# Memory attention plus SwiGLU on one core: the first step's tiles on other memory, a reciprocal kept in PSUM, a Silu call placed earlier, and a refitted order

## The chip, the cores and the metric

The kernel runs on one core of a Trainium2 chip. The time is device microseconds of one execution; the time before is the median of three runs. A profile of one execution gives the trace that is read here. The engines are named as the profile names them: PE (matmul), PEld (its weight loads), DVE (VectorE), ACT (ScalarE), POOL (GpSimd) and SP (SyncE, which issues the DMAs). Every engine executes its own queue in order.

## The reference

Sizes: 8 batches, 8 heads, 576 positions, head size 64, 32 memory slots; then 4608 tokens, model width 512, inner width 1536.

```python
a = phi - np.max(phi, axis=2, keepdims=True); a = np.exp(a)
a = a / (np.sum(a, axis=2, keepdims=True) + 1e-09)       # softmax over positions
k_m = np.einsum('bhsm,bhsd->bhmd', a, k)
v_m = np.einsum('bhsm,bhsd->bhmd', a, v)
scores = scale * np.matmul(q, k_m.transpose(0, 1, 3, 2))
attn = softmax over the 32 slots (with + 1e-09 on the sum)
x = np.matmul(attn, v_m)              # heads side by side: 4608 x 512
rms = np.sqrt(np.mean(x * x, axis=-1, keepdims=True) + 1e-06)
xn = x / rms * rms_g
out = (silu(xn @ w_gate) * (xn @ w_val)) @ w_out
```

The weights come as float64; the kernel turns them into float32 itself, and multiplies with each operand split into a high and a low float32r part.

## The kernel before, in words

The work has two parts, and the kernel never forms `x`: it multiplies the value memories with the weights first, and the attention weights with that product.

**Part 1** (the block under `with ExitStack() as c1`) does the attention. For each batch b: `prep` finds the maximum of phi and takes the exponentials into `e_bd`; `kv_steps` multiplies them with k and v into the PSUM tile `kvp` (L633), sums the exponentials by matmuls with `ones` into column 128 of the same tile (`sums`, L648), and then `post1` forms 1/sum in the small tile `si`, masks it with `hmask` into `im` and scales `kvp` by it (L656 to L665); `turn`, `post2`, `self_products` and `post3` transpose and give `km`, `vm` and the Gram matrix `gram`. For the pairs of batches 0 and 1, `q_steps` transposes q and `score_steps` makes the scores in the PSUM tiles `S` (two buffers of two banks each, last read by the subtraction in `top`, L786), their exponentials `ex` and the attention weights `a0` and `a1`. `x_steps` then transposes these (`tp`, PSUM tag "tr"), finds each row's mean square through the Gram matrix and scales the transposed weights by 1/rms into `ath` and `atl`; its scale `rp` is also a "tr" tile, read by L237. The scores of pairs 2 and 3 are made in part 2.

Beside it `convert` turns raw float64 weights into float32 (five DVE instructions, two or three on ACT, one or two on POOL) and splits them into `wh` and `wl`; chunk 0 of gate and value (`first_weights`) and chunk 1 (`second_weights`) are made in part 1. Chunk 1 lies on memory that the k, v and phi tiles leave.

**Part 2** is 48 steps. A step takes one pair of batches and one of the 12 chunks of 128 inner columns. `vw_steps` multiplies `vm` with the weights into `vp` (PSUM tag "vw", two banks, L974) and splits it to `xh` (ACT, L986) and `xl` (DVE, L987); `gv_steps` has 48 matmuls with `ath` and `atl` into `pg` and `pv` (L1010), Silu on ACT (L1018), the product `hf` on DVE (L1019) and its split `hh`, `hl`; every second step `out_steps` multiplies with the converted output weights into `po` (L1057), which is added to `acc` (L1065).

Memory: pools are laid out one after the other, tags in the order of their first request. When part 1's pools close, part 2's pools (`sb2`, `ps2`) take the same addresses. With `reuse_waits="tile"` a new tile waits only for the old tiles that it overlaps. In PSUM part 1's pool has the tags "tr" (2 banks), "kx" (2) and "S" (4), in this order; part 2's has "vw" (2), "g" (2), "v" (2) and "o" (2). So `vp` of step 0 lies on the two "tr" banks. In SBUF part 1's pool begins with `ones`, `hmask`, `a0` and `a1`, and part 2's begins with `xh` and `xl`.

Order: each step is a function with a place in a list (`ev`), and the list is sorted by numbers from the table `PRM`. What a function issues goes to a list scheduler with the place as its priority: in a timing model of its own, each engine takes the first instruction that is ready, so an instruction that is ready early can run far ahead of its place. The outcome is a fixed queue per engine. The loads of part 1 are chained (`load`) and keep their order on SP; weight conversions are kept behind the last urgent DVE instruction (`behind`). In `PRM`, `CE` says whether POOL or DVE makes `w` of the early weights, `SUM` who sums the score exponentials, `ESN` how many exponential tiles POOL adds ahead of the sums, `XE` who copies transposes; most of the rest are places in the order.

Of the kernel before, what the change touches and what calls it, by code (L numbers as in the profile page):

```python
# [19 lines left out]
WB = 4  # L20
PRM = dict(
    KB=4,
    QB=3,
    K_AT=[13.363, 15.05, 40.982, 65.819, 100.72, 121.436, 146.779, 167.28],
    KP=0.907,
    POST=[-0.317, -0.317, 4.032, 7.881, 15.383, 23.226],
    P1=4.2,
    PREP=[4.604, 5.96, 6.364, 6.4, 20.493],
    PD=[1.603, 10.918, 5.724, 18.42, 6.909, 0.895],
    EXP=[-1.616, 14.831, 1.92, 5.136, 15.121, 4.651],  # L30
    ES=1.147,
    PH=[9.097, 16.192, 41.396, 73.222, 103.794, 133.428],
    S_AT=[32.949, 48.182, 51.299, 66.888, 103.839, 110.401, 116.081, 122.952],
    KD=[-15.069, -115.131, -42.204, -7.345, -6.094, -15.243, -0.175, -2.835, -28.265, -16.354, -17.024,
        -8.311, -12.025, -12.235, -27.337, -21.619, -22.801, -22.01, -23.715, -24.999, -11.785, -13.845,
        -8.155, -10.419, -16.375, -22.685, -11.543, -19.501, -66.165, -9.755, -3.349, -20.028],
    QD=[6.956, 5.589, 2.612, 8.893, 23.53, 19.934, 25.06, 15.038],
    PD0=2.054,
    QL=3.761,
    OL=3.513,  # L40
    QO=[-1.164, 3.407, -1.815, -0.482, 0.012, 2.8],
    SO=[7.704, 15.319, 18.727, 24.931],
    X_AT=[100.47, 150.686],
    XP=1.802,
# [12 lines left out]
    RO=2.79,
    RS=5.688,
    RP=0.93,
    GV=[0.232, 0.271, 0.296, 0.752, 0.896, 1.089],  # L60
    VW=[-0.128, -0.088, 0.063],
    VW0=0.397,
    O=[0.116, 0.297, 0.448, 0.514, 0.879, 0.955, 1.365, 1.487, 1.518],
    PRE=[-0.634, 0.045, 0.27, 1.342, 2.044, 2.566],
    PRE0=[-0.813, 0.602, 1.228, 1.622, 2.25, 2.279],
    PI=0.128,
# [5 lines left out]
    XM=[22.486, 25.397],
    XN=[-0.337, -0.244, -0.081, 0.028, 0.132, 0.484, 0.518, 0.593, 0.593],
    LV=[20.239, 20.03, 20.406, 21.822],
    VD=[20.27, 15.694, 12.047, 24.508],
    U=[[-1.581, -1.57, -1.37, -1.197, -0.96, -0.96], [-1.522, -1.522, -1.12, -1.12, -1.036, -0.964], [-1.618,
        -1.5, -1.335, -1.085, -1.074, -0.071]],
# [23 lines left out]
def kernel(  # L101
# [376 lines left out]

    with ExitStack() as c1:
        sb = c1.enter_context(tc.tile_pool(name="sb1", bufs=2, reuse_waits="tile"))  # L480
        ps = c1.enter_context(tc.tile_pool(name="ps1", bufs=2, space=PSUM, reuse_waits="tile"))
        early_weights()
        c1k = ExitStack()
        sk = c1k.enter_context(tc.tile_pool(name="sbk", bufs=2, side="right", reuse_waits="tile"))

        ones = sb.tile([P, 1], F32, name="ones", bufs=1)
        nc.vector.memset(ones, 1.0)
        hmask = sb.tile([P, 2], F32, name="hmask", bufs=1)
        for g in range(4):
# [132 lines left out]
        def kv_steps(b):  # L622
# [112 lines left out]
        def q_steps(pr, s):  # L735
            def order():
                qt = st.pop(("q", pr, s))
                qr = sb.tile([P, NT, 2, 64], F32, tag="qr", name=f"qr{pr}_{s}")
                src, dst = qt.rearrange("p h (c d) -> p h c d", c=NT), qr.rearrange("p c h d -> p h c d")
                nc.scalar.copy(dst, src)  # L740
                st["qr", pr, s] = qr

            def turn(t0):
                n = min(4, NT - t0)

                def f():
                    if t0 == 0:
                        st["qT", pr, s] = sb.tile([P, NT, P], F32, tag="qT", name=f"qT{pr}_{s}")
# [16 lines left out]
        def score_steps(pr, s):  # L765
            R = 2 * NT

            def mm():
                qT = st.pop(("qT", pr, s))
                sp = ps.tile([P, 1024], F32, tag="S", name=f"S{pr}_{s}", bufs=PRM["B"][2])  # L770
                for t in range(NT):
# [9 lines left out]
            def top():  # L781
                spv = st.pop(("sp", pr, s))[:, :NT * 64].rearrange("p (r m) -> p r m", m=M)
                mxs = sb.tile([P, R, 1], F32, tag="mxs", name=f"mxs{pr}_{s}")
                nc.vector.tensor_reduce(out=mxs, in_=spv, axis=AX.X, op=ALU.max)
                ex = sb.tile([P, R, M], F32, tag="ex", name=f"ex{pr}_{s}", bufs=2)
                nc.vector.tensor_tensor(  # L786
# [8 lines left out]
            def norm():  # L795
# [5 lines left out]
                else:  # L801
# [462 lines left out]
```

## Time and profile before

| | |
|---|---|
| median of 3 runs | 883.67 us (882.39 to 885.04) |
| the profiled execution | 882.99 us; span of its instructions 881.2 us |
| mean granted TensorE clock | 0.978 |
| busy: PE, PEld, DVE, ACT, POOL | 835.1, 743.3, 547.5, 398.0, 309.7 us |
| DMA | 131.64 MB, mean 149 GB/s |

Part 1 fills about the first 140 us of the span; the first `vp` of part 2 starts at 139.88 us. Times inside the trace are counted from the span's start. "Idle before" in brackets is how long the engine stood still ahead of an instruction, and what released it. The granted clock is given as a share of full speed.

### The profile page before, as it was taken

The numbers are of one execution on the slowest core, as the hardware profiler recorded it, in microseconds if no ns is written. First come the engines' busy times: TensorE is split into PE (matmuls) and PEld (weight loads), VectorE is DVE, ScalarE is ACT, GpSimd is POOL, SyncE is SP. The second block draws the span as 40 slices with busy tenths as digits, with TensorE's granted clock in tenths as the row PEclk, the third lists the DMA queues.
The fourth block names the chain that finished last, engine by engine and source line by source line (L and its number), as shares of the span: only waits on it lengthen the run. The fifth ranks groups of instructions, "written<-read, shape, count | busy, mean of one in ns | idle before, by whom it ended". The sixth has DMA issues, their size and how long they took to land.

```text
span 881.2 us, 16498 instructions
## 1 busy us (share of the span) xinstructions
PE 835.1 (95%) x6207; PEld 743.3 (84%) x6207; DVE 547.5 (62%) x988; ACT 398.0 (45%) x709; POOL 309.7 (35%) x261
## 2 busy tenths in 40 slices
PE   5899898989999999999999999999999999999997
PEld 4787787979998978978889987979988898899896
DVE  5679684888578888897898636502443444444434
ACT  2656445767755555556545421435322323232220
POOL 2453525554534543533543621511221212122120
PEclk9989797999999999999999999999999999999999
DMA  9992934545435355344353464765645546453437
GB/s 322 326 386 72 299 110 102 154 139 147 122 78 136 119 135 149 111 122 134 115 149 102 141 155 113 192 167 133 176 103 148 133 119 173 105 148 82 90 100 169
DMA packets 110246, 131.64 MB, mean 149 GB/s; under 512 B 45140, under 2 KB 74840, under 8 KB 110168
## 3 DMA queue, kind: packets, MB, share of 16 engines
q1 hardware_dynamic: 110168, 130.60, 52.2%
q8 instruction: 49, 0.80, 0.4%
q14 instruction: 29, 0.24, 0.1%
HBM read 73.93 MB, written 31.46 MB: 120 GB/s over the span
## 4 chain that ended last, share of the span: by engine, by line
PE 65%; DVE 10%; DMA 8%; issue 6%; ACT 5%; POOL 4%; SPq 2%; ACTq 0%; POOLq 0%; DVEq 0%
PE po L1057 26%; PE pg L1010 12%; PE pv L1010 12%; PE kvp L633 3%; PE vp L974 3%; PE vq L924 2%; SPq L955 2%; POOL hl L1038 1%; DMA q<-in_q_dram 1%; PE kvp L648 1%; DMA xh<-sh 1%; ACT xh L986 1%; DVE ex L388 1%; DVE mi L418 1%; POOL w L434 1%
## 5 line engine op out<-in xcount | busy, mean ns | idle before, releaser
L1038 POOL TENSOR_TENSOR hl<-hf,hh 128x512 fp32r<-128x512 f32 (+1 forms) x86 | 125.7, 1464 | 284.6 <-ACT hh L1037 273.6
L1065 DVE TENSOR_TENSOR acc<-po,acc 128x512 f32<-128x512 f32 x180 | 123.3, 687 | 125.1 <-PE po L1057 124.0
L1057 PE MATMUL po<-oh,hh 128*128 128x512 f32 x387 | 155.7, 404 | 7.9 <-DVE acc L1065 3.0
L1057 PE MATMUL po<-ol,hh 128*128 128x512 f32 x387 | 153.0, 395 | 0.4 <-DMA xh<-sh 0.4
L1057 PE MATMUL po<-oh,hl 128*128 128x512 f32 x387 | 152.9, 395 | 0.0
L1019 DVE TENSOR_TENSOR hf<-pv,sg 128x256 f32<-128x256 f32 x192 | 84.4, 452 | 92.4 <-PE pv L1010 44.6
L1018 ACT ACTIVATE sg<-pg 128x256 f32<-128x256 f32 x192 | 77.0, 410 | 131.6 <-PE pg L1010 124.7
L1010 PE MATMUL pg<-ath,xh 128*128 128x320 f32 (+1 forms) x384 | 88.0, 302 | 6.8 <-ACT xh L986 4.4
L1057 PEld LDWEIGHTS po<-oh,hh 128*128 128x128 f32 x387 | 72.5, 188 | 23.3 <-DVE acc L1065 5.6
L1010 PE MATMUL pv<-ath,xh 128*128 128x320 f32 (+1 forms) x384 | 86.0, 300 | 1.3 <-DVE hf L1019 1.3
L1057 PEld LDWEIGHTS po<-oh,hl 128*128 128x128 f32 x387 | 72.8, 188 | 16.9
L1010 PE MATMUL pg<-ath,xl 128*128 128x320 f32 (+1 forms) x384 | 86.1, 297 | 1.0 <-DMA xl<-sl 0.9
L1010 PE MATMUL pv<-ath,xl 128*128 128x320 f32 (+1 forms) x384 | 86.5, 297 | 0.0
L1010 PE MATMUL pg<-atl,xh 128*128 128x320 f32 (+1 forms) x384 | 84.5, 296 | 0.0
L1010 PE MATMUL pv<-atl,xh 128*128 128x320 f32 (+1 forms) x384 | 84.4, 297 | 0.0
L1057 PEld LDWEIGHTS po<-ol,hh 128*128 128x128 f32 x387 | 72.9, 188 | 10.8 <-DMA ol<-od 1.6
L1037 ACT CAST hh<-hf 128x512 fp32r<-128x512 f32 (+1 forms) x86 | 57.6, 675 | 51.8 <-DVE hf L1019 38.1
L434 POOL TENSOR_TENSOR w<-mi,ex 128x512 f32<-128x512 f32 x34 | 43.9, 1291 | 91.1 <-ACT mi L425 56.7
L1010 PEld LDWEIGHTS pg<-ath,xh 128*128 128x128 f32 x384 | 64.5, 189 | 13.1 <-ACT xh L986 5.2
L987 DVE TENSOR_TENSOR xl<-vp,xh 64x1024 fp32r<-64x1024 f32 x48 | 58.5, 1219 | 18.5 <-ACT xh L986 17.8
L1010 PEld LDWEIGHTS pg<-ath,xl 128*128 128x128 f32 x384 | 64.4, 190 | 4.0 <-DMA xl<-sl 1.1
L1010 PEld LDWEIGHTS pv<-ath,xh 128*128 128x128 f32 x384 | 63.2, 190 | 4.8 <-DVE hf L1019 1.8
(148 smaller groups left out, 1540.3 us busy)
## 6 DMA issues: line engine op xcount, KB each, us to landing
xh<-sh SPq DMA_DIRECT2D x192, 64.0 KB, 2.1
xl<-sl SPq DMA_DIRECT2D x192, 64.0 KB, 2.0
out_dram<-acc SPq DMA_DIRECT2D x72, 128.0 KB, 2.4
raw<-in_moe_w_gate_dram SPq DMA_DIRECT2D x12, 512.0 KB, 4.0
raw<-in_moe_w_val_dram SPq DMA_DIRECT2D x12, 512.0 KB, 3.6
wd<-wh SPq DMA_DIRECT2D x24, 256.0 KB, 3.5
wd<-wl SPq DMA_DIRECT2D x24, 256.0 KB, 3.6
raw<-in_moe_w_out_dram SPq DMA_DIRECT2D x12, 512.0 KB, 3.6
```

What stands on the lines that cost most here:

```text
L434: (nc.gpsimd if on_pool else V).tensor_tensor(out=d["w"], in0=m, in1=ex, op=ALU.mult)
L633: nc.tensor.matmul(kvp[64 * par:64 * par + 64, cc, 0:128], e_bd[j][:, hp, c, :], st["kv", b, hp][:, :, 64 * c:64 * c + 64], start=(c == 0) ...
L924: nc.tensor.matmul(vp[:, h, e, :], vall[a][:, cc, k:k + 4, :].rearrange("p q m -> p (q m)"), w, start=(a == 0), stop=(a == 1),)
L974: nc.tensor.matmul(vp[:, cc, e, :], lhs(l), r[:, 2 * cc + e, :], start=(n == 0), stop=(n == 2),)
L987: urgent.append(nc.vector.tensor_tensor(out=xl[rows], in0=src, in1=xh[rows].bitcast(F32), op=ALU.subtract).ins)
L1010: nc.tensor.matmul(pt[:, :N], l[cc][:, b, half * P:half * P + P], r[:, cc, b, t0:t0 + n, :].rearrange("p t x -> p (t x)"), start=(m == 0), ...
L1018: nc.scalar.activation(sg[:, :N], pg[:, :N], AF.Silu)
L1019: urgent.append(nc.vector.tensor_tensor(out=hf[:, :, b, :], in0=pv[:, :N].rearrange("p (t x) -> p t x", x=64), in1=sg[:, :N].rearrange("p ...
L1037: nc.scalar.copy(hh, hv)
L1038: nc.gpsimd.tensor_tensor(out=hl, in0=hv, in1=hh.bitcast(F32), op=ALU.subtract)
L1057: nc.tensor.matmul(po, l[:, tt, :], r, start=(m == 0), stop=(m == 5))
L1065: nc.vector.tensor_tensor(out=accs[key], in0=po, in1=accs[key], op=ALU.add).ins
```

## The change

- **Pools.** A new SBUF pool `sb1a` lies ahead of `sb1` and holds `a0`, q, `qr`, `qT` and `ex`. A new PSUM pool `ps1s` with the "S" tiles lies ahead of `ps1`. `ones`, `hmask` and `rg` move to the persistent pool; `a1` is allocated when it is first written.
- **PSUM tags of part 2.** `pg` and `pv` get the tags "g0", "g1", "v0", "v1" with one buffer each, so that the banks in order are vw (2), g0, v0, g1, v1, o (2).
- **1/sum.** `si` is no tile of its own any more but column 129 of `kvp`.
- **Silu.** One activation with Silu on `ones` is placed at 150 in the order.
- **Order.** New numbers in `PRM`. The ones that change who does what: `CE[0]` 2 to 3 (POOL instead of DVE makes `w` of gate chunk 0), `SUM[1]` 0 to 2 (POOL instead of DVE sums one of eight score tiles), `ESN[6]` 0 to 1 (POOL adds two tiles ahead of batch 6's sums, 8 matmuls fewer), `XE[3]` 17 to 21 (one copy of pair 3 from DVE to ACT).

```diff
 PRM = dict(
+    DS=150,
...
-    K_AT=[13.363, 15.05, 40.982, 65.819, 100.72, 121.436, 146.779, 167.28],
-    KP=0.907,
-    POST=[-0.317, -0.317, 4.032, 7.881, 15.383, 23.226],
-    P1=4.2,
-    PREP=[4.604, 5.96, 6.364, 6.4, 20.493],
+    K_AT=[13.363, 15.05, 40.982, 64.708, 100.72, 121.436, 147.13, 167.28],
+    KP=0.88,
+    POST=[-0.317, -0.206, 4.032, 7.881, 15.383, 23.226],
+    P1=4.084,
+    PREP=[4.511, 5.867, 6.271, 6.307, 20.4],
...
-    EXP=[-1.616, 14.831, 1.92, 5.136, 15.121, 4.651],
+    EXP=[-9.517, 14.262, 1.741, 4.567, 14.552, 4.082],
...
-    CE=[2, 2],
-    XE=[12, 11, 29, 17],
-    ESN=[2, 3, 2, 0, 3, 1, 0, 1],
-    SUM=[2, 0, 1, 0, 0, 1, 2, 1],
+    CE=[3, 2],
+    XE=[12, 11, 29, 21],
+    ESN=[2, 3, 2, 0, 3, 1, 1, 1],
+    SUM=[2, 2, 1, 0, 0, 1, 2, 1],
...
     with ExitStack() as c1:
+        sa = c1.enter_context(tc.tile_pool(name="sb1a", bufs=2, reuse_waits="tile"))
         sb = c1.enter_context(tc.tile_pool(name="sb1", bufs=2, reuse_waits="tile"))
+        ps_s = c1.enter_context(tc.tile_pool(name="ps1s", bufs=2, space=PSUM, reuse_waits="tile"))
         ps = c1.enter_context(tc.tile_pool(name="ps1", bufs=2, space=PSUM, reuse_waits="tile"))
...
-        ones = sb.tile([P, 1], F32, name="ones", bufs=1)
+        ones = persist.tile([P, 1], F32, name="ones")
-        hmask = sb.tile([P, 2], F32, name="hmask", bufs=1)
+        hmask = persist.tile([P, 2], F32, name="hmask")
-        a_tiles = [sb.tile([P, NT, 256], F32, name=f"a{i}", bufs=1) for i in range(G)]
+        a_tiles = {0: sa.tile([P, NT, 256], F32, name="a0", bufs=1)}
-        rg = [sb.tile([P, HP], F32, name=f"rg{i}", bufs=1) for i in range(2)]
+        rg = [persist.tile([P, HP], F32, name=f"rg{i}") for i in range(2)]
...
-            t = sb.tile([P, 2, S], F32, tag="q", name=f"q{pr}_{s}", bufs=PRM["QB"])
+            t = sa.tile([P, 2, S], F32, tag="q", name=f"q{pr}_{s}", bufs=PRM["QB"])
...
-                si = sb.tile([P, 2, 1], F32, tag="si", name=f"si{b}")
+                si = kvp[:, :, 129:130]
...
-                sp = ps.tile([P, 1024], F32, tag="S", name=f"S{pr}_{s}", bufs=PRM["B"][2])
+                sp = ps_s.tile([P, 1024], F32, tag="S", name=f"S{pr}_{s}", bufs=PRM["B"][2])
...
+                if pr not in a_tiles:
+                    a_tiles[pr] = sb.tile([P, NT, 256], F32, name=f"a{pr}", bufs=1)
...
         ev += place(PRM["CV"], [PRM["CP"] * i for i in range(len(w))], w)
+        ev.append((PRM["DS"], lambda: nc.scalar.activation(
+            sb.tile([P, 1], F32, name="warm", bufs=1), ones, AF.Silu)))
...
-                    pg = ps.tile([P, 512], F32, tag="g", name=f"pg{i}_{gi}{b}")
-                    pv = ps.tile([P, 512], F32, tag="v", name=f"pv{i}_{gi}{b}")
+                    pg = ps.tile([P, 512], F32, tag=f"g{b}", name=f"pg{i}_{gi}{b}", bufs=1)
+                    pv = ps.tile([P, 512], F32, tag=f"v{b}", name=f"pv{i}_{gi}{b}", bufs=1)
```

The tiles `qr`, `qT` and `ex` of part 1 move to `sa` in the same way as q. The other changed numbers of `PRM` are places in the order, most of them by less than one unit.

More of the change, by code (lines that the diff above doesn't have):

```diff
@@ L21 @@
 PRM = dict(
+    DS=150,
     KB=4,
     QB=3,
-    K_AT=[13.363, 15.05, 40.982, 65.819, 100.72, 121.436, 146.779, 167.28],
-    KP=0.907,
-    POST=[-0.317, -0.317, 4.032, 7.881, 15.383, 23.226],
-    P1=4.2,
-    PREP=[4.604, 5.96, 6.364, 6.4, 20.493],
+    K_AT=[13.363, 15.05, 40.982, 64.708, 100.72, 121.436, 147.13, 167.28],
[3 more added lines that the diff above has]
+    PREP=[4.511, 5.867, 6.271, 6.307, 20.4],
     PD=[1.603, 10.918, 5.724, 18.42, 6.909, 0.895],
-    EXP=[-1.616, 14.831, 1.92, 5.136, 15.121, 4.651],
-    ES=1.147,
+    EXP=[-9.517, 14.262, 1.741, 4.567, 14.552, 4.082],
+    ES=1.541,
     PH=[9.097, 16.192, 41.396, 73.222, 103.794, 133.428],
-    S_AT=[32.949, 48.182, 51.299, 66.888, 103.839, 110.401, 116.081, 122.952],
+    S_AT=[32.949, 48.182, 51.299, 66.888, 103.621, 110.401, 116.081, 122.952],
     KD=[-15.069, -115.131, -42.204, -7.345, -6.094, -15.243, -0.175, -2.835, -28.265, -16.354, -17.024,
@@ L36 @@
         -8.155, -10.419, -16.375, -22.685, -11.543, -19.501, -66.165, -9.755, -3.349, -20.028],
-    QD=[6.956, 5.589, 2.612, 8.893, 23.53, 19.934, 25.06, 15.038],
-    PD0=2.054,
+    QD=[7.122, 5.589, 2.612, 8.893, 23.53, 19.934, 25.06, 15.038],
+    PD0=1.045,
     QL=3.761,
     OL=3.513,
[L41 to L44, printed above, removed]
+    QO=[-1.164, 3.407, -1.815, -0.482, 0.012, 2.591],
+    SO=[7.743, 14.98, 18.206, 24.112],
+    X_AT=[100.536, 150.686],
+    XP=1.796,
     LAG=0.891,
-    CV=112.01,
+    CV=111.332,
     CP=3.361,
     CV2=160.133,
-    CP2=1.082,
+    CP2=1.09,
     QE=[4, 0],
-    CE=[2, 2],
-    XE=[12, 11, 29, 17],
-    ESN=[2, 3, 2, 0, 3, 1, 0, 1],
-    SUM=[2, 0, 1, 0, 0, 1, 2, 1],
+    CE=[3, 2],
+    XE=[12, 11, 29, 21],
+    ESN=[2, 3, 2, 0, 3, 1, 1, 1],
+    SUM=[2, 2, 1, 0, 0, 1, 2, 1],
     CA=1,
@@ L57 @@
     RO=2.79,
[L58 to L66, printed above, removed]
+    RS=6.461,
+    RP=0.555,
+    GV=[0.232, 0.246, 0.274, 0.752, 0.884, 1.089],
+    VW=[-0.104, -0.023, 0.07],
+    VW0=0.373,
+    O=[0.116, 0.297, 0.452, 0.514, 0.874, 0.991, 1.365, 1.487, 1.518],
+    PRE=[-0.635, 0.045, 0.27, 1.342, 2.044, 2.566],
+    PRE0=[-0.813, 0.784, 1.109, 1.622, 2.25, 2.293],
+    PI=0.13,
     PSW=[1.981, 2.035, 1.951, 2.415, 3.159, 3.803],
-    SU=[1.874, 3.101, 5.773, 6.557, 9.723, 12.208, 13.41, 15.533],
-    AO=[0.214, 0.237, 0.237, 0.276, 0.394, 0.423, 0.543, 0.581, 0.621, 0.621, 0.621, 0.819, 1.065, 1.397],
+    SU=[1.877, 3.104, 5.776, 6.56, 9.726, 12.211, 13.413, 15.536],
+    AO=[0.214, 0.237, 0.237, 0.276, 0.397, 0.423, 0.543, 0.581, 0.621, 0.621, 0.621, 0.819, 1.065, 1.397],
     XB=[17.199, 22.761],
     XS=[0.1086, 0.0359],
[L72 to L77, printed above, removed]
+    XM=[22.138, 25.161],
+    XN=[-0.302, -0.244, -0.092, 0.028, 0.161, 0.484, 0.518, 0.593, 0.603],
+    LV=[20.282, 20.03, 20.406, 21.652],
+    VD=[29.86, 23.48, 21.637, 34.098],
+    U=[[-1.581, -1.578, -1.37, -1.197, -0.96, -0.96], [-1.522, -1.522, -1.12, -1.12, -1.036, -0.964], [-1.618,
+        -1.5, -1.335, -1.003, -1.003, -0.071]],
     RL=[-1.906, -3.752, -5.714],
-    RW=[1.932, 0.852],
+    RW=[1.932, 0.552],
     CB=1,
@@ L737, in order @@
                 qt = st.pop(("q", pr, s))
-                qr = sb.tile([P, NT, 2, 64], F32, tag="qr", name=f"qr{pr}_{s}")
+                qr = sa.tile([P, NT, 2, 64], F32, tag="qr", name=f"qr{pr}_{s}")
                 src, dst = qt.rearrange("p h (c d) -> p h c d", c=NT), qr.rearrange("p c h d -> p h c d")
@@ L747, in f @@
                     if t0 == 0:
-                        st["qT", pr, s] = sb.tile([P, NT, P], F32, tag="qT", name=f"qT{pr}_{s}")
+                        st["qT", pr, s] = sa.tile([P, NT, P], F32, tag="qT", name=f"qT{pr}_{s}")
                     qr = st["qr", pr, s]
@@ L784, in top @@
                 nc.vector.tensor_reduce(out=mxs, in_=spv, axis=AX.X, op=ALU.max)
-                ex = sb.tile([P, R, M], F32, tag="ex", name=f"ex{pr}_{s}", bufs=2)
+                ex = sa.tile([P, R, M], F32, tag="ex", name=f"ex{pr}_{s}", bufs=2)
                 nc.vector.tensor_tensor(
```

## Prediction

> **What bounds the kernel now.** I read the page first, then busy time by stretches of 4 us, then the stretch around the change from part 1 to part 2 engine by engine. The page:
>
> ```profile
> span 881.2 us, 16498 instructions
> PE 835.1 (95%) x6207; PEld 743.3 (84%) x6207; DVE 547.5 (62%) x988; ACT 398.0 (45%) x709; POOL 309.7 (35%) x261
> PEclk9989797999999999999999999999999999999999
> ```
>
> PE is busy 95% of the span, so 881.2 - 835.1 = 46.1 us is all that PE waits. The clock row, where a digit is a fortieth (22 us), shows less than full clock only in the first seven fortieths: what waiting and half clock cost early is found in part 1 and its end. The profiled execution took 882.99 us, 1.79 us more than its span; the median 883.67 lies 0.68 above that.
>
> Busy time by stretches (start:end, length, busy us and count of PE, PEld, DVE, ACT, POOL, then granted clock):
>
> ```profile
> 84.00:88.00 4.00, 2.35 (x39) 1.67 (x35) 4.00 (x11) 1.56 (x4) 2.01 (x3) 1.00 0.01 2
> 92.00:96.00 4.00, 2.15 (x16) 1.32 (x12) 3.74 (x15) 2.10 (x3) 1.81 (x5) 0.98 0.92 216
> 96.00:100.00 4.00, 1.68 (x22) 1.68 (x24) 0.00 (x0) 1.56 (x3) 1.16 (x1) 0.87 0.98 365
> 136.00:140.00 4.00, 3.41 (x22) 2.22 (x20) 3.73 (x8) 1.82 (x5) 1.12 (x3) 0.56 0.00 0
> 140.00:144.00 4.00, 2.81 (x12) 2.51 (x12) 0.12 (x1) 2.99 (x7) 4.00 (x4) 0.58 0.71 180
> 144.00:148.00 4.00, 1.80 (x10) 1.80 (x11) 2.89 (x4) 1.01 (x1) 2.49 (x4) 0.84 0.80 216
> 148.00:152.00 4.00, 4.00 (x28) 4.00 (x26) 2.25 (x5) 3.40 (x6) 1.29 (x1) 0.73 0.67 116
> 180.00:200.00 20.00, 16.30 (x97) 13.82 (x98) 16.47 (x23) 14.35 (x24) 10.68 (x8) 1.00 0.49 142
> ```
>
> From 136 to 152 us PE is busy for 12.0 of 16 us at 0.56 to 0.84 of its clock; from 92 to 100 for 3.8 of 8. Later idle stretches are single ones (3.70 us in 180 to 200). PE's own order shows what it waits for (the bracket is the idle time ahead of a row, and its releaser):
>
> ```profile
> 98.32 3.32 PE L633 MATMUL kvp<-kv,e_bd 128*64 128x128 f32 x33 [3.50 <-DMA kv<-in_v_dram]
> ...
> 138.42 0.47 PE L229 MATMUL rp<-ident,rinv 128*128 128x128 f32 x1 [0.28 <-DVE at L237]
> 139.88 0.58 PE L974 MATMUL vp<-wh,vm 128*128 128x256 f32 x1 [0.31 <-DVE at L237]
> ...
> 146.20 0.51 PE L1010 MATMUL pg<-ath,xh 128*128 128x256 f32 x2 [3.39 <-ACT xh L986]
> ...
> 149.79 0.57 PE L1010 MATMUL pv<-ath,xl 128*128 128x256 f32 x2
> ...
> 157.21 0.40 PE L1010 MATMUL pg<-ath,xh 128*128 128x256 f32 x2
> ```
>
> The first `vp` of part 2 waits for the DVE's L237 and then runs at half clock, PE stands still for 3.39 us until `xh` is there, and `pg` and `pv` of step 0 run at half clock until about 150.1 (4 us from 146.20). Step 1's `pg` begins at 157.21; I use that row as the mark by which the two kernels are compared. The hole ahead of 98.32 is another matter: a v tile of batch 5 that could not be loaded earlier; the change leaves the load's place (`KD`) as it is.
>
> **What the first step waits for, and what is left of it.** The DVE and POOL rows that decide:
>
> ```profile
> 89.58 0.75 DVE L786 TENSOR_TENSOR ex<-S,mxs 128x576 f32<-128x576 f32 x1
> ...
> 110.97 0.76 DVE L786 TENSOR_TENSOR ex<-S,mxs 128x576 f32<-128x576 f32 x1
> ...
> 137.16 2.67 DVE L237 TENSOR_TENSOR at<-at,rp 128x1024 f32<-128x1024 f32 x3
> ```
>
> ```profile
> 89.33 1.27 POOL L452 TENSOR_TENSOR wl<-w,wh 128x512 fp32r<-128x512 f32 x1 [0.73 <-ACT wh L451]
> ...
> 141.95 1.27 POOL L452 TENSOR_TENSOR wl<-w,wh 128x512 fp32r<-128x512 f32 x1
> ```
>
> Before, `vp` lies on the "tr" banks, whose last reader is the group of L237 that ends at 139.83. After, it lies on the first of the "S" buffers, whose last reader is the seventh score tile's L786 at 89.58 to 90.33; its weights' last piece `wl` is ready at 90.60. So `vp` of step 0 can start from about 91 us, and `xh`, `xl` on `a0` and q, dead by then, can follow at once (DVE is idle from 96 to 100). `pg` and `pv` of the first half lie on the other S buffer, free at 111.73, and those of the second half still on "tr". As the scheduler gives every engine whatever is ready, this work goes wherever PE has nothing else.
>
> That it runs instructions far ahead of their place is seen here: the copy of `gram` to `gb` for pair 0 has place 100.3 (`X_AT` less a tenth of `XP`), batch 1's `gram` has 43.7, and the copy ran 0.28 us behind it.
>
> ```profile
> 38.44 0.25 ACT L716 COPY gram<-kvt 128x128 f32<-128x128 f32 x1
> 38.72 0.82 ACT L198 COPY gb<-gram 64x256 f32<-64x256 f32 x2
> ```
>
> **The sum.** Term by term, against 882.99:
>
> The idle ahead of `pg` is removed: -3.39. The wait of `vp` for L237: -0.31; that of `rp` (0.28) stays, it lies on "tr" still. `vp` itself took 2.94 us there at half clock and 1.44 at full clock:
>
> ```profile
> 139.88 2.94 PE vp L974 x12
> 142.85 1.02 ACT xh L986
> 143.88 1.23 DVE xl L987
> ...
> 158.79 1.44 PE vp L974 x12
> ```
>
> In the hole of 3.50 us ahead of 98.32 it fits even at 2.94, and costs nothing: -2.94. The cover is the missing v tile; without the hole it costs 1.44 to 2.94 again, so this term lies between 0 and -2.94, and I take the end, since the hole's load keeps its order. Half clock from 146.20 to 150.1 costs half of 3.9 us, 1.95. It ends earlier if PE is kept busy from 137 on, but the sums before 136 and the rest of part 1 are still short matmuls: between 0 and -1.95, I take -1.0. Together -7.6.
>
> A second chain could hold the mark back: step 1's `vp` needs the `wl` that POOL ends at 143.22. Then 1.44 for `vp` and the 3.39 from `vp` to `pg`: 148.05, which is 9.2 us ahead of 157.21. That does not bind.
>
> [...]
>
> **What is handed back.** PE comes some 7 us early to the weight conversions. DVE is busy for 16.47 us of the 20 from 180 to 200, and PE waits 3.70 there. DVE has room ahead of that: 0.27 + 3.88 + 1.11 + 1.75 = 7.0 us idle in the four stretches from 136 to 152, and two `xl` (2.45) move out of them; the conversion of the first output weights, which is kept behind `xl`, can move up into that room. So most of the gain can hold. The ends are 0 and +3.7 (the wait of that later stretch once more); I take +1.0.
>
> **Moves that I cost at nothing.** 1/sum in PSUM: 3 DVE instructions for each of 8 batches now write or read PSUM. Nearest rows, PSUM to PSUM against PSUM to SBUF at 128x256:
>
> ```profile
> L284 DVE CUSTOM_DVE_ANT_0 xp<-xp,a 128x256 f32<-128x256 f32 x18 | 7.6, 429 | 1.7 <-PE xp L271 1.6
> ...
> L1148 DVE TENSOR_TENSOR ex<-S,mx 128x256 f32<-128x256 f32 x8 | 3.3, 416 | 0.1
> ```
>
> 13 ns more each, 0.3 us in all if every one were on the path; only batch 7's three are: 0.04. The other end, a cheaper write, is -0.3. The tags g0 to v1 keep the alternation of two buffers each; `ones`, `hmask`, `rg` change address only.
>
> Silu. The only table load ahead of Exp, the first Silu's load, and the last Exp of part 1:
>
> ```profile
> 3.88 1.28 ACT L602 ACT_TABLE_LOAD   x1 [3.88 <-DMA phi<-in_phi_dram]
> ...
> 117.11 2.34 ACT L602 ACTIVATE e_bd<-phi 64x1152 f32<-64x1152 f32 x2 [2.35 <-DVE phi L592]
> ...
> 149.82 1.28 ACT L1018 ACT_TABLE_LOAD   x1
> ```
>
> The new activation needs only `ones`, written in the first microsecond, so like the `gram` copy it will run at the front of ACT's queue; Exp is then loaded anyway at 3.88, in ACT's idle time, and the Silu load at 149.82 stays: 0. Ends: -1.28 if it came between the last Exp and the first Silu and the load was on the path; +2.56 if it ran just ahead of an Exp of batch 6 or 7 and both loads were on the path.
>
> POOL instead of DVE for `w` of gate chunk 0 takes one of these out of a stretch in which DVE is 4.00 of 4 busy and PE waits (84 to 88):
>
> ```profile
> 76.40 0.42 DVE L413 TENSOR_SCALAR mi<-raw 128x512 int32<-128x512 int32 x1
> ...
> 80.90 1.01 DVE L434 TENSOR_TENSOR w<-mi,ex 128x512 f32<-128x512 f32 x1
> ...
> 83.17 1.50 DVE L413 TENSOR_SCALAR mi<-raw 128x512 int32<-128x512 int32 x1
> ```
>
> ```profile
> 82.98 1.42 POOL L452 TENSOR_TENSOR wl<-w,wh 128x512 fp32r<-128x512 f32 x1 [0.39 <-ACT wh L451]
> ```
>
> -1.01 at most. But L413 took 0.42 at 76.40 and 1.50 at 83.17, beside a POOL instruction; a further POOL instruction of 1.3 us there can cost +1.08. I take 0 between these. [...] `SUM`, `ESN` and `XE` move work of the same size between engines that wait there; the other places shift what runs where by an amount that no row shows. I bound all that by the largest late idle stretch, won or lost once: 3.70 either way, and take 0.
>
> Sum: -7.6 + 1.0 = -6.6, so 876.4 for the profiled execution and 877.1 at the median. I predict 877.
>
> **The rivals.**
>
> *The gain is handed back at DVE.* PE is early, but `hf`, `xl` and the conversions from 150 to 200 are not. For it: 16.47 of 20 us. Against it: the idle DVE from 136 to 148. Price: +3.7 in place of +1.0, so 883.67 - 3.9 = 879.8; with a slightly worse order it falls into the middle band.
>
> *Slower: work of step 0 stands in PE's queue ahead of part 1's and waits.* The scheduler's model, not the chip, decides where `pg` of step 0 stands. If it stands among the batch 6 or pair 1 work from 108 to 129 and `xh`, `xl` are late on the chip, PE stops there as it did ahead of 146.20: 3.39, and then half clock for 3.9 us, 1.95: 5.3 us a time, on the chain that part 1 depends on. Once leaves -6.6 + 5.3 = -1.3; from the second time it is slower: 883.67 - 6.6 + 10.6 = 887.7. For it: PE's queue is in order, and a late load already holds it for 3.50 ahead of 98.32. Against it: after that hole `xl` has some 10 us to spare, until the second S buffer is free at 111.73.
>
> *The tiles do not come to lie so, or the model leaves the work where it was.* Then the handover stays, and only the refitted places act: 883.67 with 3.70 to either side.
>
> *The Silu stands late, ahead of the last Exp:* 877.1 + 2.6 = 879.7, still faster.
>
> **How the numbers follow.** The forecast, with the late Silu as a variant in it, has 0.66, and its own range is 871 to 881: with the clock at -1.95 and nothing handed back the sum gives 875.1, with a won stretch 871.4; with a lost one the forecast's 877.1 becomes 880.8. Handed back at DVE 0.15, slower by waiting 0.11, unchanged 0.08. A measurement can tell about 0.3% from no change here: faster is below 881.0, slower above 886.3. Of the rival at DVE I count half as faster, of the unchanged one a little on each side: faster 0.75, same 0.14, slower 0.11. The range for 8 in 10 goes from 870 to 885: it takes in the unchanged handover and the DVE rival, and leaves out the slower one and the far tail below.
>
> **What would show it.** In the changed kernel `vp` of step 0 stands before 100 us, or at least before the last sums; the idle of 3.39 ahead of the first `pg` is gone; the stretches from 136 to 152 show PE near 4 of 4 busy and full clock from about 142; step 1's `pg` begins near 150. The first Silu's table load is still there, beside a new one at the start. From 160 to 200 PE's idle grows by about 1 us, not 4. I am wrong if step 0's `vp` still follows L237, if PE shows a new wait for `xh` or `xl` inside part 1, or if the mark moves by 7 us and the end does not.

## The result and the profile after

The changed kernel takes 879.59 us (median of 16 runs, 875.54 to 882.89); the kernel before took 883.44 us beside it (16 runs, 879.5 to 889.34). The ratio is 0.9945 with an interval from 0.9923 to 0.9968: 4.9 us faster, by 2.8 to 6.8. (The means of the 16 runs give the same 0.9945; the medians differ by 3.9 us.) A ratio leaves out a run that lies over 1.5% above the fastest of its kernel, which happened once, in *numbers and 1/sum in PSUM* below (888.55 us). I had predicted 877.0, between 870 and 885, and faster. The sign and the range hold; the profiled execution even came out at the 876.4 us of my sum. It did so by another route than the sum's, and most of this section and the next is about that.

The page of the changed kernel:

```profile
span 874.6 us, 16472 instructions
PE 826.1 (94%) x6191; PEld 737.7 (84%) x6191; DVE 541.1 (62%) x985; ACT 398.4 (46%) x712; POOL 315.3 (36%) x268
PEclk9999797999999999999999999999999999999999
```

Span minus PE's busy time is 48.5 us, against 46.1 before. PE does not wait less. It is busy for 9.0 us less, with the same matmuls but for the 8 that `ESN[6]` saves (two records each: 6191 against 6207). Those are batch 6's sums, which take 2.90 us of PE in place of 3.85. What the page offers for part of the rest is the clock: the granted mean is 0.982 against 0.978.

PE's order at the two places that the prediction spoke of. Columns: start, length, then the instructions; in brackets the idle time ahead and what ended it:

```profile
92.74 2.61 PE L636 MATMUL kvp<-kv,e_bd 128*64 128x128 f32 x22 [2.90 <-DMA kv<-in_v_dram]
...
132.89 0.70 PE L710 MATMUL kvt<-vt 128*64 128x64 f32 x8
133.52 0.58 PE L981 MATMUL vp<-wh,vm 128*128 128x256 f32 x1
...
139.83 0.50 PE L1017 MATMUL pg<-ath,xh 128*128 128x256 f32 x2 [3.38 <-ACT xh L993]
...
150.38 0.40 PE L1017 MATMUL pg<-ath,xh 128*128 128x256 f32 x2
```

Here the forecast's mechanism falls. Step 0's `vp` has lost its wait, as the new tiles allow, but it did not move. It stands right behind part 1's last transposes (`kvt` from `vt`), and not in the hole ahead of 92.74. The idle time ahead of `pg` is 3.38 us, against 3.39 before. From `vp` to the first `pg` it is 6.31 us, against 6.32. Of the handover only the 0.31 us of `vp`'s wait is gone.

The mark, step 1's `pg`, is nevertheless at 150.38 in place of 157.21, 6.8 us earlier. But a second profile of the same changed kernel has it here:

```profile
104.86 0.48 PE L680 MATMUL kvt<-ident,kb 128*128 128x128 f32 x1
...
136.84 0.38 PE L981 MATMUL vp<-wh,vm 128*128 128x256 f32 x1
...
142.73 0.59 PE L1017 MATMUL pg<-ath,xh 128*128 128x256 f32 x2 [4.21 <-ACT xh L993]
...
153.27 0.40 PE L1017 MATMUL pg<-ath,xh 128*128 128x256 f32 x2
```

The mark moves by 2.9 us between two executions of one program, so one pair of profiles cannot say what an edit is worth here. The lead of 6.8 us has two parts, one that is the change and one that is chance. (0.4 us of it is order: four `qtp` records that stood ahead of the mark now stand behind it.) The stretches around 45 us show the part that is chance. Up to there PE's queue is the same in both kernels, and yet batch 2's transposes start at 48.37 us before, at 44.84 in the changed kernel's first profile, and at 47.45 in its second. Columns: start and end, length, busy time of PE, PEld, DVE, ACT and POOL, granted clock, DMA share and GB/s. The kernel before, the changed kernel, and its second profile:

```profile
40.92:44.34 3.42, 3.30 (x64) 3.08 (x59) 2.27 (x3) 3.37 (x5) 0.00 (x0) 1.00 1.05 391
44.34:47.75 3.41, 3.41 (x30) 2.63 (x32) 1.69 (x7) 2.53 (x4) 2.09 (x5) 0.50 1.06 383
47.75:51.16 3.41, 3.41 (x73) 2.88 (x71) 2.21 (x6) 1.67 (x6) 1.85 (x3) 1.00 1.07 384
```

```profile
44.97:48.38 3.41, 3.41 (x68) 2.95 (x69) 3.00 (x8) 1.82 (x6) 2.30 (x4) 1.00 1.05 379
```

```profile
44.01:47.42 3.41, 3.41 (x40) 2.88 (x40) 1.28 (x5) 2.12 (x3) 2.51 (x6) 0.50 1.04 380
```

In the kernel before, PE runs at exactly half clock from 44.34 to 47.75 and does 30 matmuls there, against 73 in the next 3.41 us. The changed kernel does not have this stretch in its first profile, and has it in its second. In the first 160 us the kernel before drew 37.5 us of half clock, the changed kernel 27.3 in one profile and 34.1 in the other. In the kernel before, step 0's `vp` took 2.94 us at half clock and step 1's 1.44 at full clock; from these I estimate that half clock costs half of its length where PE is busy throughout, and the first pair's difference of 10.2 us is worth up to 5.1 us. This is one reason why the first profile pair can show more (6.6 us) than the 16 runs each do (4.9).

Part 2 varies too. From the mark to the end of the span it is 723.99 us before, 724.22 and 720.63 in the two profiles of the changed kernel. PE's waits for the output weights account for 2.6 of the 3.6 us between the last two (tile and line, the releaser, then total, count and longest). First profile, from 150 us on:

```profile
PE po L1064 <- DMA oh<-od: 3.0, 3, 1.2
PE po L1064 <- DMA ol<-od: 2.1, 1, 2.1
```

Second profile:

```profile
PE po L1064 <- DMA oh<-od: 1.6, 2, 0.8
PE po L1064 <- DMA ol<-od: 0.9, 2, 0.5
```

The two rows hold 5.1 and 2.5 us.

### The profile page after: what moved, and what is told of

It reads as the page before. It is cut to its first block, busy times and chain, and to the rows that moved or that the text cites. A ratio compares the mean times of both kernels' runs of the same rounds, so it can differ in the third digit from the quotient of the medians.

```text
span 874.6 us, 16472 instructions
## 1 busy us (share of the span) xinstructions
PE 826.1 (94%) x6191; PEld 737.7 (84%) x6191; DVE 541.1 (62%) x985; ACT 398.4 (46%) x712; POOL 315.3 (36%) x268
## 4 chain that ended last, share of the span: by engine, by line
PE 71%; DVE 11%; DMA 5%; issue 4%; ACT 4%; POOL 3%; SPq 2%; POOLq 0%; ACTq 0%; DVEq 0%
PE po L1064 28%; PE pg L1017 14%; PE pv L1017 14%; PE vp L981 3%; PE vq L931 3%; PE kvp L636 2%; DMA q<-in_q_dram 1%; DVE ex L389 1%; POOL w L435 1%; PE kvp L651 1%; DVE mi L419 1%; DVE acc L1072 1%; POOL hl L1045 1%; DVE ex L392 1%; DVE xl L994 1%
## 5 line engine op out<-in xcount | busy, mean ns | idle before, releaser
L1064 PEld LDWEIGHTS po<-ol,hh 128*128 128x128 f32 x387 | 73.3, 189 | 11.9 <-DMA ol<-od 2.9
```

Of the source, the lines that this page charges most:

```text
L1064: nc.tensor.matmul(po, l[:, tt, :], r, start=(m == 0), stop=(m == 5))
```

## The experiments

Ratios are to the kernel before, run on the same chip beside each.

| kernel | ratio | interval | median us |
|---|---|---|---|
| changed kernel | 0.9945 | 0.9923 to 0.9968 | 879.59 |
| the same again | 0.9966 | 0.9939 to 0.9993 | 878.74 |
| numbers of `PRM` alone | 0.9980 | 0.9958 to 1.0003 | 881.25 |
| the same again | 0.9989 | 0.9968 to 1.0010 | 882.2 |
| all but the numbers | 0.9971 | 0.9944 to 0.9997 | 880.12 |
| the same again | 0.9967 | 0.9942 to 0.9992 | 880.28 |
| numbers and 1/sum in PSUM | 0.9919 | 0.9892 to 0.9946 | 878.55 |
| Silu call alone | 1.0012 | 0.9985 to 1.0039 | 882.72 |
| changed, without the Silu call | 0.9945 | 0.9912 to 0.9977 | 877.27 |
| changed, Silu call behind the last Exp | 0.9983 | 0.9961 to 1.0005 | 882.63 |
| changed, batch 5's last loads earlier | 1.0011 | 0.9985 to 1.0037 | 883.3 |
| changed, step 0's `vp` issued in part 1 | 0.9947 | 0.9922 to 0.9973 | 878.27 |
| the same, q loads ahead of others | 0.9944 | 0.9916 to 0.9973 | 876.46 |

### The change in two halves

My theory was the prediction's: the memory edits carry the gain. Its rival: the numbers carry it. *Numbers alone* is the kernel before with the changed table and no Silu call (two of the changed places):

```diff
-    K_AT=[13.363, 15.05, 40.982, 65.819, 100.72, 121.436, 146.779, 167.28],
+    K_AT=[13.363, 15.05, 40.982, 64.708, 100.72, 121.436, 147.13, 167.28],
...
-    CE=[2, 2],
+    CE=[3, 2],
```

> The kernel before with the whole table PRM of the changed kernel (without the place of the Silu call) and nothing else: pools, PSUM tags, 1/sum and Silu stay as before. Theory 'numbers' (the whole gain comes from the refitted places and assignments): the ratio of the changed kernel, 0.9945 (878.6 us against 883.44), within 0.001; in its trace step 1's first pg near 150.5 and the first vp near 133.5 with at most 0.3 us of wait for L237 ahead of it. Theory 'memory' (the gain comes from tiles on other addresses): 1.000, 883.4 us. Theory 'clock' (the two profiled runs differ mainly by how many half-clock stretches each happened to draw in part 1, 11 before and 8 after, and the order is worth little): between 0.995 and 1.000, and the trace again shows another set of half-clock stretches.

*All but the numbers* is the changed kernel with the table of before (pools, tags, 1/sum and the Silu call stay):

> The changed kernel with the table PRM of before (and the Silu call at 150): pools, PSUM tags, 1/sum in PSUM and the Silu call as changed, every engine's order as before except the Silu call at the front of ACT. Theory 'numbers': 0.9995 to 1.000 (at most 0.31 us for vp's wait for L237), about 883.2 us, and the idle of 3.4 us ahead of the first pg is still there. Theory 'memory': 0.9945, 878.6 us. My prediction's mechanism (vp floats into the hole near 98 us, 3.4 us of idle gone) would be 0.992 to 0.994 here; by the order of its queue vp stays behind the last kvt, so I do not expect it.

And the changed kernel once more beside them:

> The changed kernel unchanged, to set beside the other three on the same chip, and as a second trace of the same program. Theory 'numbers': 0.9945 again, and in the trace the same early lead as in the first (kvt of batch 1 at 27.6 against 29.6 before, kvt of batch 2 at 44.8 against 48.4), as it comes from the order. Theory 'clock': the order is the same in both kernels up to about 48 us, so the lead of 3.5 us at 44.8 is not the change's; this trace shows kvt of batch 2 anywhere between 44.8 and 48.4, and half-clock stretches at other times than the first trace.

The numbers alone give 0.9980, the rest 0.9971, the changed kernel 0.9966. The intervals overlap, so I ran both halves again:

> The kernel before with the changed kernel's numbers, a second time, to halve the interval (0.9958 to 1.0003 the first time). Theory 'numbers carry the gain': 0.996 or below. Theory 'a clean share of each': 0.998.

> The changed kernel with the numbers of before, a second time (0.9944 to 0.9997 the first time). By its queues only vp's wait for L237 (0.31 us) can go, so theory 'numbers': 0.9995 to 1.000. If it is 0.997 again, the memory edits do something that the order of the queues does not show.

They gave 0.9989 and 0.9967. The two means are 0.9985 and 0.9969, which are 1.3 and 2.7 us; multiplied they give 0.9954, between the two ratios of the changed kernel. So the halves add up within the uncertainty, and the memory half is the larger one by its means; each interval of its two runs excludes 1, and neither interval of the numbers does. This half has an instructive property: its queues hold the same instructions in the same order as those of the kernel before, but for the Silu call at ACT's front. Whatever it gains, it gains without an instruction having moved. Two things differ: the wait of `vp`, 0.31 us, and where the operands lie.

### What the memory half gains by

An instruction that I had passed over in the profile of before shows it. `im` is the mask times 1/sum, four elements wide. In DVE's order of the kernel before, four of its eight rows:

```profile
61.11 0.47 DVE L659 TENSOR_TENSOR im<-si,hmask 128x4 f32<-128x4 f32 x1
...
71.69 0.31 DVE L659 TENSOR_TENSOR im<-si,hmask 128x4 f32<-128x4 f32 x1
...
106.47 0.92 DVE L659 TENSOR_TENSOR im<-si,hmask 128x4 f32<-128x4 f32 x1
...
118.15 0.36 DVE L659 TENSOR_TENSOR im<-si,hmask 128x4 f32<-128x4 f32 x1
```

POOL's order of the same kernel:

```profile
70.72 1.27 POOL L614 TENSOR_TENSOR es<-e_bd 128x512 f32<-128x512 f32 x1 [3.21 <-ACT e_bd L602]
...
117.33 1.16 POOL L813 TENSOR_TENSOR a<-ex,sm 128x576 f32<-128x576 f32 x1 [3.85 <-DVE sm L812]
```

The second `im` ends at 72.00 and POOL's `es` at 71.99; the last `im` ends at 118.51 and POOL's `a` at 118.49. The other long ones end in the same way, 0.01 to 0.03 us behind a POOL instruction that was already running. The remaining four take 0.15 to 0.16 us. The sums of all eight, by groups of instructions on DVE (count, then total and mean ns of one, then idle time ahead): the kernel before, numbers alone, and the changed kernel:

```profile
L659 DVE TENSOR_TENSOR im<-si,hmask 128x4 f32<-128x4 f32 x8 | 2.7, 336 | 0.2
```

```profile
L660 DVE TENSOR_TENSOR im<-si,hmask 128x4 f32<-128x4 f32 x8 | 3.7, 468 | 0.2
```

```profile
L662 DVE TENSOR_TENSOR im<-kvp,hmask 128x4 f32<-128x4 f32 x8 | 1.3, 159 | 0.2
```

With 1/sum in SBUF both inputs of `im` lie there, and the group takes 2.7 to 3.7 us in four profiles. With 1/sum in PSUM it takes 1.3 us in all ten, and no single one takes more than 0.16. Every long `im` (0.31 to 1.18 us in place of 0.16) began behind the POOL instruction that it ends with, and none with one input in PSUM was held: at 57.30, 66.40, 101.45 and 111.78 in the changed kernel a POOL instruction ran beside `im`, which took 0.15 or 0.16 us. By what mechanism the long ones were held, no run shows.

The excess, 1.4 us before and 2.3 to 2.5 with the numbers alone, lies on a chain: sums, 1/sum, `im`, `kb` and `vb`, their transposes on PE. But in the profile of before PE waits for none of the eight `kb`, so the time may come back through what stands behind `im` in DVE's queue; by which wait it reaches the end no row shows. Two runs test whether it is this edit. First the Silu call alone, to take it out of the memory half; it is the kernel before with

```diff
+        ev.append((150, lambda: nc.scalar.activation(
+            sb.tile([P, 1], F32, name="warm", bufs=1), ones, AF.Silu)))
```

> The kernel before with one line more: the Silu call on ones, placed at 150, which runs at the front of ACT's queue (0.73 to 2.2 us) as in the changed kernel; every other engine's order is the same. So far the kernels with that call at the front were at 0.9945, 0.9966 (the changed kernel), 0.9971 and 0.9967 (memory edits with the old numbers), those without it at 0.998 and 0.9989 (numbers only) and 0.9983 (the call moved behind the last Exp). Theory 'the call at the front carries the gain of the memory edits': 0.997. Theory 'the tiles' addresses carry it' or 'chance': 1.000, since nothing in the trace waits for or gains by that call.

1.0012: the Silu call gives nothing. Then *numbers alone* with this one edit of memory, and neither pools nor tags:

```diff
-                si = sb.tile([P, 2, 1], F32, tag="si", name=f"si{b}")
+                si = kvp[:, :, 129:130]
```

> The kernel before with the changed kernel's numbers and 1/sum in column 129 of kvp; pools, PSUM tags and Silu stay as before. In every trace with 1/sum in SBUF so far (before, silu_only, numbers_only twice) three or four of the eight im instructions (im<-si,hmask) take 0.31 to 1.18 us in place of 0.16 and end 0.01 to 0.03 us behind a POOL instruction that runs beside them: 1.4 us too much in all with the old numbers, 2.3 to 2.5 with the new; with 1/sum in PSUM all eight take 0.15 or 0.16, in seven traces. Theory '1/sum in PSUM carries the gain of the memory edits': 0.9985 less about 0.0028, so 0.995 to 0.997, as the changed kernel; no im over 0.2 us. Theory 'pools and PSUM tags carry it': 0.998 to 0.999, though im is short.

0.9919, where the numbers alone had 0.9980 and 0.9989, with the same order on PE, DVE, POOL and SP; `im` takes 1.3 us again. The ratio stands on five runs; the median of all six (878.55 us, against 884.22 beside it) gives 0.9936. From 0.9985 it is 5.8 us to the first and 4.3 to the second, with an uncertainty of about 3 us from the intervals, and the memory half, which holds the same edit, gave 2.7. The trace's excess of 2.3 to 2.5 us sits at the low end of the first two and close to the last. That the edit shortens `im` is shown, by all ten profiles that have it; that it makes the kernel faster is what these runs say together; whether it is worth 2.5 or 5 us is not settled. For the new pools and PSUM tags no gain is left that these runs could tell: the kernel with them is at 0.9945, the one without at 0.9919. They were not run by themselves.

### The Silu call

The changed kernel runs it at the front, ahead of Exp's table. ACT's order there and at part 2's first Silu:

```profile
0.73 1.28 ACT L880 ACT_TABLE_LOAD   x1 [0.73 <-PEq L1255]
2.02 0.20 ACT L880 ACTIVATE warm<-ones 128x1 f32<-128x1 f32 x1
3.83 1.28 ACT L605 ACT_TABLE_LOAD   x1 [1.60 <-DMA phi<-in_phi_dram]
...
143.45 1.28 ACT L1025 ACT_TABLE_LOAD   x1
144.75 0.66 ACT L1025 ACTIVATE sg<-pg 128x256 f32<-128x256 f32 x2
```

So the load ahead of the first Silu, at 143.45, stays. One end of the prediction's range said that the call would be worth 1.28 us between the last Exp and the first Silu. I put the call behind part 1's last Exp:

```diff
+        def warm():
+            with tc.issue_after(exps[-1]):
+                nc.scalar.activation(sb.tile([P, 1], F32, name="warm", bufs=1), ones, AF.Silu)
+
+        ev.append((169.0, warm))
```

> The changed kernel with the Silu call pinned behind part 1's last Exp on ACT, where ACT has idle time, in place of the front of ACT's queue; every other engine's order is the same. The Silu table is then loaded near 114 us and the first sg of part 2 has no load ahead of it. Theory 'the load at 143.45 is covered, PE has other matmuls until 146': 0 us, ratio as the changed kernel's, 0.9945 to 0.997, and step 1's first pg still 10.5 us behind step 0's. Rival 'the load is on the path': -1.28 us, and that distance becomes 9.3.

0.9983: nothing gained, and by its mean slower than the changed kernel (the intervals overlap). Its ACT order, and the row of PE that follows from it:

```profile
115.26 2.34 ACT L605 ACTIVATE e_bd<-phi 64x1152 f32<-64x1152 f32 x2 [2.35 <-DVE phi L595]
117.61 1.28 ACT L882 ACT_TABLE_LOAD   x1
118.91 0.20 ACT L882 ACTIVATE warm<-ones 128x1 f32<-128x1 f32 x1
119.02 0.57 ACT L220 COPY at<-tp 128x512 f32<-128x512 f32 x1
```

```profile
119.64 1.98 PE L272 MATMUL xp<-gb,at 128*64 128x128 f32 x16 [0.98 <-ACT at L220]
```

The load now stands ahead of the copy of `at`, and PE waits 0.98 us for it. Just ahead of that it waits 0.81 us for POOL; the two waits together are 1.79 us, against 1.53 and 1.76 in the two profiles of the changed kernel, so these rows show next to no loss. Nothing comes back at the other end: step 1's `pg` starts 10.5 us behind step 0's with the load at 143.45 as without it, so PE's other matmuls cover that load. Without the call at all,

```diff
-        ev.append((PRM["DS"], lambda: nc.scalar.activation(
-            sb.tile([P, 1], F32, name="warm", bufs=1), ones, AF.Silu)))
```

> The changed kernel without the Silu call; all else is the same, the order of PE, DVE, POOL and SP too. Theory 'the call at the front carries the gain of the memory edits': 0.9985 as numbers only. Theory 'addresses': 0.9955 as the changed kernel (0.9945 and 0.9966). Theory 'the Silu call is worth nothing', my prediction's: the same.

the kernel has 0.9945, the changed kernel's own ratio. The call is worth nothing where it is.

### The forecast's mechanism, put there by hand

Is it true that an early `vp` removes the idle time ahead of `pg`? I issued step 0's `vp`, `xh` and `xl` in part 1's own list, on the S tile as the change has it, behind the sums of batch 6; `qr` and `qT` share a pool with part 2's `xl` and `xh`:

```diff
+        sx = ctx.enter_context(tc.tile_pool(name="sbx", bufs=2, reuse_waits="tile"))
...
+            vp0.append(ps_s.tile([P, 1024], F32, tag="S", name="vp0", bufs=PRM["B"][2]))
...
+                        with tc.issue_after(last["sum", 6]):
+                            nc.tensor.matmul(
...
+        ev += [(159.5, early_mm), (176.5, early_split)]
...
-    ev = place(-1.0, PRM["VW"], vw_steps(0))
```

> The changed kernel, with step 0's vp, xh and xl issued from part 1's own list: vp takes an S tile and stands on PE behind the sums of batch 6, just ahead of the first tp of pair 1, which waits 1.53 us for POOL there; the two xh stand on ACT behind the copy of batch 6's gram (5.18 us idle behind it), the two xl on DVE behind the last rinv (3.46 us idle behind it). qr and qT share the memory of xl and xh. This does what I predicted of the change: vp out of the handover and no idle ahead of the first pg. Theory 'the forecast's mechanism is worth what I reckoned, only the change did not bring it about': the idle of 3.4 to 4.2 us ahead of pg goes, vp's 1.5 to 2.9 us go into a hole, the first pg starts within 0.5 us of the last kvt; against the changed kernel -5 to -7 us, 872 to 874 us, ratio to the kernel before 0.989 to 0.991. Rival 'the gain is handed back': step 1's xh, xl or wl, or DVE at 150 to 200 us, holds PE instead; less than 2 us is left, 0.9945 to 0.997.

PE's order of this kernel:

```profile
115.77 0.39 PE L893 MATMUL vp<-wh,vm 128*128 128x256 f32 x1
...
139.22 0.69 PE L712 MATMUL kvt<-vt 128*64 128x64 f32 x8 [1.36 <-ACT vt L696]
139.84 0.58 PE L1048 MATMUL pg<-ath,xh 128*128 128x256 f32 x1
...
149.67 0.50 PE L1048 MATMUL pg<-ath,xh 128*128 128x256 f32 x2
...
154.72 0.52 PE L1157 MATMUL qtp<-ident,qr 128*128 128x128 f32 x3 [2.88 <-DMA qr<-in_q_dram]
```

`vp` is 23 us ahead of the handover, and the first `pg` follows the last `kvt` with no idle time. From batch 5's transposes of `kb` (107.08 here) to step 1's `pg` it is 42.6 us, against 47.5 and 48.4 in the two profiles of the changed kernel. Seven matmul records that stood ahead of the mark now stand behind it (four of `qtp`, three of `po`, about 1 us), so I count records as well: when PE has 1665 of them behind it, the same work in each kernel, it is 38.7 us from batch 5's `kb` against 42.8 and 43.8. So the mechanism is real, and worth 4 to 5 us there, part of it less half clock (7.9 us between `kb` and the mark, against 13.7 and 10.8). Note that `pg`, whose inputs were ready at 133.3, still stands behind part 1's last transposes: instructions issued in part 2 did not pass the end of part 1's list in any of these kernels.

Yet the time is 0.9947. The last row above holds the answer for this kernel: PE, early, finds q of pair 2 not there, waits 2.88 us, and then runs 3.4 us at half clock. Counted in matmul records, at 1800 of them, it stands 62.3 us behind batch 5's `kb`, against 61.5 and 62.5 in the changed kernel: the lead is gone. The q loads were issued at 149.48, behind others on SP. I kept those others back:

```diff
+                    with tc.issue_after(pins["q", G, 0]):
+                        nc.sync.dma_start(
```

> The kernel with step 0's vp in part 1 (early_vp), with one thing more: the loads of vgl (L1127) are kept behind the first loads of q for pair 2 on SP. In early_vp's trace PE stood 2.88 us at 154.72 for that q, issued at 149.48, which the earlier start of part 2 had uncovered, and ran 3.4 us at half clock behind it; all other engines' orders stay. Theory 'the rest of the forecast's gain was lost there': q is issued 1.3 us earlier or more, the wait falls to about 1.5 us, and the half-clock stretch may go: 0.3 to 3 us less than early_vp's 0.9947, 0.992 to 0.994. Rival 'it is lost elsewhere in part 2': 0.9947 again.

```profile
152.93 0.63 PE L1158 MATMUL qtp<-ident,qr 128*128 128x128 f32 x4 [0.65 <-DMA qr<-in_q_dram]
```

The wait falls to 0.65 us, the path from batch 5 stays short (43.1 us), and the ratio is 0.9944. On the same chip the changed kernel without its Silu call has 0.9945. So 2.2 of the 2.88 us of that one wait were recovered and do not show in the time. The count of records tells where they go: at 1800 this kernel is 2.2 to 3.1 us ahead of the two profiles of the changed kernel, at 4000 (496 us of its span) still 2.4 to 3.3, and at 4800 1.3 ahead of the one and 0.6 behind the other. Over those 800 records PE waits 5.1 us for DMAs of weights and of `xl` and draws one piece of half clock. The changed kernel waits 5.0 us for such DMAs there in one profile and 2.6 in the other, so whether the early `vp` brings these waits about is open. No version came out faster than the changed kernel beyond the uncertainty.

### The hole ahead of batch 5's tile

The prediction had put `vp` into the hole that a late v tile of batch 5 leaves. What if the tile is loaded earlier?

```diff
-        -8.155, -10.419, -16.375, -22.685, -11.543, -19.501, -66.165, -9.755, -3.349, -20.028],
+        -8.155, -10.419, -16.375, -22.685, -11.543, -19.501, -20.0, -9.755, -3.349, -20.028],
```

> The changed kernel with one number more changed: KD[28] from -66.165 to -20, so that the first k and v tile of batch 7 no longer takes one of the four kv buffers ahead of batch 5's last tile. In the queue of SP batch 5's last tile and batch 6's loads then stand ahead of the stores of wh and wl (L464), which wait for POOL. Theory 'the hole of 2.90 us ahead of kvp at 92.74 is set by that load, issued only at 86.14 behind those stores': the hole goes and PE, which is busy 0.47 of 4 us from 88 to 92 and 3.26 at half clock from 92 to 96, gains 3 to 6 us: 873 to 876 us, ratio 0.988 to 0.992. Rival 'DVE sets the end of that stretch' (4.00 busy of 4 from 76 to 84): the time comes back as waits for DVE or POOL, at most 1 us gained, 0.994.

1.0011, so nothing gained, and by its mean the changed kernel's gain is lost (the interval touches that of the changed kernel's second run). The trace is of the slowest of its 12 runs (890.01 us), so I read the order of the waits in it and not their sizes. The tile is issued at 63.40 in place of 86.14 and the wait for it is gone, but PE's order and the stretches of this kernel show another wait in its place:

```profile
89.12 0.79 PE L272 MATMUL xp<-gb,at 128*64 128x128 f32 x8 [2.89 <-DVE ssq L285]
```

```profile
84.00:88.00 4.00, 1.70 (x23) 1.03 (x18) 4.00 (x5) 1.41 (x3) 2.38 (x3) 1.00 0.09 33
88.00:92.00 4.00, 2.46 (x24) 2.09 (x26) 4.00 (x14) 1.67 (x4) 1.78 (x2) 0.69 0.01 2
92.00:96.00 4.00, 4.00 (x57) 3.66 (x55) 4.00 (x9) 1.60 (x3) 2.63 (x4) 0.88 0.79 210
```

DVE is busy for 12.0 of 12 us there, and in the changed kernel for 11.9 of the 12 from 76 to 88. That fits the rival, by which DVE sets the stretch with or without the tile; what else is lost here no run shows.

## Why the prediction was right, and where it was wrong

- **The step that failed:** "As the scheduler gives every engine whatever is ready, this work goes wherever PE has nothing else." The freed memory makes `vp` ready at about 86 us in the changed kernel (the seventh score tile is last read until 85.09, the last `wl` ends at 85.57), and the row at 133.52 shows that it did not go there. The `gram` copy that I gave as evidence ran ahead of its place inside part 1's list; for an instruction issued in part 2 it proved nothing. With it fall the terms -3.39 (3.38 is still there), -2.94 for `vp` in the hole (it still runs behind `kvt`, 2.93 us long at half clock in the first profile), and -1.0 for the clock from 146 on (a piece of 3.41 us of half clock, from 140.54, stands there still). That half clock ends earlier when PE is kept busy, which the term -1.0 and the full clock expected from about 142 suppose, no run shows; in the first profile of the changed kernel the granted clock is 0.50 from 140.54 to 143.95 and 1.00 from there to 152. Of the handover -0.31 came true. Why the scheduler holds part 2's instructions back, no run shows.
- **That failure was named:** "the model leaves the work where it was", with a chance of 0.08 and the price of the numbers alone. Its mechanism is what happened, and its "only the refitted places act" is wrong too.
- **1/sum in PSUM** I had at 0.3 us either way, from what access to PSUM costs. That cost is there: the instruction that makes the sum takes 0.165 us in place of 0.157, the reciprocal 0.177 in place of 0.165. But the term was mis-sized, since I looked at what the new operand costs and not at what the old one had cost: 1.4 us of held `im` in the profile of before, 2.7 us in the runs of the memory half, more in the last test. For `CE` I had weighed just such rows (L413 took 0.42 us at 76.40 and 1.50 at 83.17, beside a POOL instruction), and had not looked for them in this small instruction.
- **The refitted order** was taken at 0 within 3.70 either way; it measured -1.3 us, which is inside the bounds and not clear of nothing (both intervals contain 1). `CE`, `SUM`, `ESN` and `XE` were not tried one by one, so no run shows what each is worth.
- **Silu at 0** was right, and so was its reason: it runs at the front, and the old load stays. Behind the last Exp, where one end of the range had a gain of 1.28 us, the call gained nothing; ahead of the last Exp, priced at +2.6 us, it was not tried.
- **Handed back**, +1.0 (0 to 3.7): the changed kernel has nothing to hand back at the handover. Where the handover was really shortened, by 4 to 5 us, the time of the runs shows none of it. I had named DVE as the place; the rows show loads instead (2.88 us for q, and later waits for weights).
- **The number.** My sum of -6.6 from removed stalls met a profile of -6.6, for which the runs and rows offer less half clock, a shorter `im` and the refitted numbers, while the runs say -4.9. That the sum met the one profile is luck, and it would have looked like a proof; that the time lies in the range owes nothing to the handover either. The sum also read 3.9 us of half clock behind 146.20, where the clock records have one piece of 3.41, from 146.74 to 150.15. What I had listed as signs of being right (no idle time ahead of `pg`, `vp` before 100) decided it, and not the mark near 150, which did come true.

## What to carry to other kernels

In a group of very short instructions read the longest one and not the mean: here a four-element instruction of 0.92 us beside others of 0.16 ended with a POOL instruction beside it, and with one operand moved to another memory it took 0.16 at most, without any instruction having moved. Memory that is free earlier makes an instruction ready earlier, but it runs earlier only if the order lets it pass what stands ahead; check in the queue. Before you explain a difference of a few microseconds between two profiles, profile one of the kernels twice, and compare them at an equal count of matmul records: a mark moves with the order.

## What the runs showed of the hardware that I had not expected

**The half clock came in whole pieces.** In all 14 profiles the stretches of half clock in the first 160 us last 3.41, 6.83, 10.24, 13.65 or 17.07 us, multiples of 3.413, and within one execution they all start on one grid of 3.413 us (before, from 17.04 to 146.74, it is 38 steps). The grid's phase differs from execution to execution: 3.38 us before, 0.59 and 3.05 in the two profiles of the changed kernel. How much half clock an execution draws differs too: 27.3 and 34.1 us for one and the same program, between 23.9 and 44.4 over these kernels. What makes a piece half I could not settle: in the profile of before PE shows no pause in the 3.41 us ahead of the piece at 61.41 (busy for 3.41 of 3.41 us at a granted clock of 1.00). My term for the clock counted 3.9 us of half clock in one place and half of it saved. The pieces by which two profiles differ are whole ones of 3.41 us, worth up to 1.7 us each, and they may lie far from any edit: that at 44.34, before, is 92 us ahead of the handover.

**A short DVE instruction was held until a POOL instruction ended.** `im` of 0.16 us took up to 0.92 us in the kernel before, each long one ending 0.01 to 0.03 us behind POOL's instruction. With one of its two inputs in PSUM it never took over 0.16 us, beside the same POOL work.
